# Attention outputs placed inside a retention visit, and other PSUM banks for the first and last batch

## The chip, the cores and the metric

The kernel runs on one core of a Trainium2 chip. What is measured is the device time of one execution in microseconds (us). The engines are named as in the profile: PE is TensorE (matmuls), PEld its weight loads, DVE is VectorE, ACT is ScalarE, POOL is GpSimd, and SP issues the DMAs. Matmul results lie in PSUM, which has 8 banks; everything else lies in SBUF.

## What is computed

Three stages run over 8 batches of 576 positions, all in float32. Cut to what matters, the reference is:

```
# retention: 8 heads of 64
ret = (q @ k.T) / 8 * D           # D[i,j] = gamma**(i-j) for i >= j, else 0
x = (ret @ v)                      # laid out as (8, 576, 512)
# mixture of attentions: 4 experts, the best 2 of each position are kept
logits = x @ w_gate
for e in range(4):
    a = softmax(causal(x @ wq[e] @ (x @ wk[e]).T / 8))
    ye = a @ (x @ wv[e]) @ wo[e]
    out += (gate weight of e at this position, or 0) * ye
# token and channel mixing
theta = out @ w_theta
y = w_tok_r @ (out * cos(theta)) + w_tok_i @ (out * sin(theta))
u = out + y
return u + relu(u @ w_ch)
```

## The kernel before

**First half** (to about 485 us). Retention is done in chunks of 128 positions, each of two blocks of 64. A visit, `ret_step(b, c, nx)`, does the late part of chunk c and the early part of the next chunk: `ret_scores` (line 134), `ret_state` (line 150: the running state, summed in the one PSUM bank `pS`, which ACT copies to S in line 153 after each block) and `ret_values` (line 163, and in line 170 the query products, which read S). All these are 64x64 matmuls on the four quarters of the array; a "diag" list (scores and states) and an "off" list (values) are taken one by one in turn, so that neighbours run at the same time. The state of an even block is the last of the diag list. It adds to pS, so it can't start before ACT has copied pS after the odd block before it.

The main loop goes through 80 units of attention (8 batches, 2 pairs of experts, 5 row tiles). A unit does `at_scores` (line 304), softmax on DVE and ACT (lines 307 and 312) and `at_trans` (line 351; DVE and ACT copy the result to PT in lines 356 and 358). `at_out` (line 370) multiplies PT with V for a group of row tiles, and ACT copies that to ob (line 374). A table, `SLOTS`, names the retention visits R1 to R5 to the next batch, made in 5 of the 10 units of a batch; the outputs that are due (`outs`) come behind a visit, in R1, R3, R4 and R5. The order of PE in this half is the order in which the code is written; the other engines' order is made by a scheduler.

At the end of the first half `token_tile` makes x2 and theta for tiles of 128 positions (lines 547 to 552; k, then nr = k minus theta in line 552, whose operand lies in pS or a w bank), and `load_o` loads the attention's outputs and multiplies them with the gate on POOL (line 520).

**Second half.** A scheduler orders all engines. `z_tile` makes z from nr for one tile and one half of the columns: three small DVE instructions (absolute value in line 564, minus pi/2 in line 565, clamp in line 566), one Sin on ACT over both halves of the tile (line 567), a product with x2 on DVE (line 569), and a split into a rounded part zh (ACT, line 103) and a rest zl (DVE, line 104). `mix(b, h)` multiplies z with the token weights TK: 108 matmuls of line 711 per half into four banks called acc, each 256 or 320 columns wide (`TS`). DVE copies or adds the banks to u (line 725 for batch 0, 723 for others), ACT makes the rounded uh (line 726), POOL or DVE the rest ul (line 727). `channel(b, et)` makes 24 matmuls for each of four blocks et (lines 98 to 100) into four banks called w, and DVE applies relu and adds to u (line 740). The loop over b also calls `x_put` (a DVE transpose, line 751, and DMAs) and `x_get` (DMAs), which lay x out anew for u.

PSUM holds, in the second half, 4 acc banks and 4 w banks. Where batch 0 goes from half 0 to half 1, half 1 has to wait until half 0 has been read out of acc.

## Time and profile before

| | us |
|---|---|
| median of 3 runs | 912.73 |
| lowest and highest | 907.61, 915.47 |
| the profiled execution | 907.77 |
| its span, first to last instruction | 905.8 |
| PE busy | 863.0 |
| DVE busy | 628.8 |
| ACT busy | 454.9 |
| POOL busy | 218.9 |

A timeline row gives the start in us from the span's start, the length in us, engine, line, operation, what is written <- what is read, how many like instructions in a row it stands for (xN), and in brackets the idle time ahead of it on its engine with what ended it. Matmuls follow each other before the one ahead has ended, so the time of a row xN is not the sum of its parts. The clock is the granted TensorE clock as a share of its full 2.4 GHz.

### The profile page before, as it was taken

To read this page: it belongs to the slowest core of one execution; us is meant where nothing else is said; L and a number is where in the kernel's file an instruction comes from. 1 tells how busy PE (TensorE), PEld (TensorE's weight loads), DVE (VectorE), ACT (ScalarE), POOL (GpSimd) and SP (SyncE) were. 2 spreads that over 40 slices of the span, in tenths; PEclk is the share of its full clock that TensorE was granted. 3 is DMA by queue.
4 is the path that set the end of the run, shared out by engine and by line. 5 is a ranking of instruction groups with operands and counts; after the bars stand their busy time and mean duration, and the time that the engine had idled before them with its cause. 6 is when DMAs were issued, how large, how long until landed. Compare 5 with 4: busy or idle time off the path is not lost.

```text
span 905.8 us, 25503 instructions
## 1 busy us (share of the span) xinstructions
PE 863.0 (95%) x10062; PEld 803.9 (89%) x10062; DVE 628.8 (69%) x1779; ACT 454.9 (50%) x1198; POOL 218.9 (24%) x268
## 2 busy tenths in 40 slices
PE   6998999899999999998999989999999999999998
PEld 6987888788898888888878889999999999999998
DVE  5376767878787776777769947866578764676732
ACT  2466666666666665665656513443244533434320
POOL 2434152452535434242212102001020110001010
PEclk8999999999999999999999999999999999999999
DMA  7857566676667667656795152333425123251401
GB/s 276 237 143 234 159 203 170 187 223 184 194 182 241 167 180 227 163 148 207 202 317 173 30 143 50 62 90 92 128 50 135 35 72 80 37 125 25 106 23 53
DMA packets 146216, 130.30 MB, mean 144 GB/s; under 512 B 83504, under 2 KB 121648, under 8 KB 146096
## 3 DMA queue, kind: packets, MB, share of 16 engines
q1 hardware_dynamic: 145952, 128.39, 50.1%
q8 instruction: 79, 1.29, 0.6%
q0 software_dynamic: 144, 0.28, 0.2%
q14 instruction: 41, 0.34, 0.1%
HBM read 78.03 MB, written 32.00 MB: 121 GB/s over the span
## 4 chain that ended last, share of the span: by engine, by line
PE 67%; DVE 10%; DMA 8%; ACT 6%; issue 3%; POOL 2%; SPq 2%; DVEq 0%; ACTq 0%; POOLq 0%
PE acc L711 22%; PE w L99 9%; PE w L98 9%; PE w L100 9%; PE w L242 4%; PE w L370 4%; PE w L304 3%; DMA kv<-kv 3%; PE w L351 2%; ACT P L312 2%; PE pS L150 2%; DVE P L307 1%; DMA TK<-td 1%; DMA wst<-w 1%; ACT U L225 1%
## 5 line engine op out<-in xcount | busy, mean ns | idle before, releaser
L711 PE MATMUL acc<-TK,zh 128*128 128x256 f32 (+1 forms) x1024 | 180.7, 299 | 3.4 <-ACT zh L103 1.8
L711 PEld LDWEIGHTS acc<-TK,zh 128*128 128x128 f32 x1024 | 155.7, 191 | 4.0 <-issue 3.7
L312 ACT ACTIVATE P<-P,st 128x128 f32<-128x128 f32 (+4 forms) x160 | 95.6, 598 | 55.9 <-DVE st L307 55.5
L711 PE MATMUL acc<-TK,zl 128*128 128x256 f32 (+1 forms) x512 | 110.9, 298 | 0.0
L727 POOL TENSOR_TENSOR ul<-u,uh 128x576 fp32r<-128x576 f32 x16 | 24.3, 1540 | 336.4 <-ACT uh L726 336.4
L307 DVE CUSTOM_DVE_ANT_0 P<-w,cm 128x128 f32<-128x128 f32 (+4 forms) x160 | 71.8, 477 | 24.4 <-PE w L304 24.1
L711 PEld LDWEIGHTS acc<-TK,zl 128*128 128x128 f32 x512 | 87.0, 191 | 0.0
L103 ACT ACTIVATE zh<-cs 128x512 fp32r<-128x512 f32 x64 | 40.4, 631 | 90.2 <-PE acc L711 68.2
L99 PE MATMUL w<-xl,WH 128*128 128x288 f32 x256 | 75.9, 296 | 4.5 <-POOL xl L183 4.5
L567 ACT ACTIVATE cs<-cs 128x512 f32<-128x512 f32 x72 | 45.2, 631 | 69.1 <-DVE cs L565 55.2
L98 PE MATMUL w<-uh,CH 128*128 128x256 f32 (+1 forms) x256 | 75.5, 297 | 2.4 <-ACT uh L726 2.4
L98 PE MATMUL w<-xh,WH 128*128 128x288 f32 x256 | 76.0, 297 | 0.7 <-ACT PT L356 0.7
L104 DVE TENSOR_TENSOR zl<-cs,zh 128x512 fp32r<-128x512 f32 x64 | 44.0, 690 | 46.4 <-ACT zh L103 45.7
L304 PE MATMUL w<-KK,U 128*64 128x288 f32 (+4 forms) x384 | 76.2, 327 | 0.0
L99 PE MATMUL w<-ul,CH 128*128 128x256 f32 (+1 forms) x256 | 75.7, 296 | 0.0
L100 PE MATMUL w<-uh,CH 128*128 128x256 f32 (+1 forms) x256 | 75.6, 296 | 0.0
L100 PE MATMUL w<-xh,WL 128*128 128x288 f32 x256 | 75.4, 295 | 0.0
L150 PE MATMUL pS<-vp,kv 64*64 64x64 f32 x1024 | 44.0, 226 | 19.8 <-ACT S L153 15.9
L442 POOL TENSOR_TENSOR r<-r,ex 128x192 f32<-128x192 f32 (+1 forms) x51 | 29.5, 579 | 136.4 <-ACT hl L443 61.8
L569 DVE SCALAR_TENSOR_TENSOR cs<-cs,x 128x512 f32<-128x512 f32 x72 | 48.7, 687 | 18.6 <-ACT cs L567 18.4
L304 PEld LDWEIGHTS w<-KK,U 128*128 128x128 f32 (+1 forms) x384 | 53.9, 171 | 7.5 <-issue 4.3
L150 PEld LDWEIGHTS pS<-vp,kv 64*64 64x64 f32 x1024 | 35.8, 137 | 27.1 <-ACT S L153 18.5
(140 smaller groups left out, 2267.2 us busy)
## 6 DMA issues: line engine op xcount, KB each, us to landing
KK<-KN SPq DMA_DIRECT2D x128, 144.0 KB
kt<-qk SPq DMA_DIRECT2D x32, 512.0 KB
kv<-kv SPq DMA_DIRECT2D x32, 512.0 KB
raw<-wd SPq DMA_DIRECT2D x43, 192.0 KB
xd<-xb SPq DMA_DIRECT2D x126, 64.0 KB
out<-u SPq DMA_DIRECT2D x28, 288.0 KB
u<-xd SPq DMA_DIRECT2D x28, 288.0 KB
td<-hl SPq DMA_DIRECT2D x27, 192.0 KB
```

Source lines behind the costliest of these rows:

```text
L98: nc.tensor.matmul(ps, ah, bh, start=first, stop=False)
L99: nc.tensor.matmul(ps, ah, bl, start=False, stop=False)
L100: nc.tensor.matmul(ps, al, bh, start=False, stop=last)
L103: nc.scalar.activation(h, src, AF.Copy)
L104: nc.vector.tensor_sub(l, src, h)
L150: nc.tensor.matmul(pS[half(s), x, :], u[half(s), j, 0, x * D:x * D + D], vp[half(s), j, x, :], start=k == 0 and x == 0, stop=False, skip_g ...
L304: nc.tensor.matmul(ps[s][:R], U[:, s, rs], KK[:, s, x, j0:j1], start=x == 0, stop=x == 1)
L307: MARK["dve"] = nc.vector.tensor_tensor_reduce(Ps[s][:R, j0:j1], ps[s][:R], cm[:R, o + j0:o + j1], 1.0, st[:R, 0, s:s + 1] if i else 3.0e3 ...
L312: MARK["act"] = nc.scalar.activation(Ps[s][:R, :n], Ps[s][:R, :n], AF.Exp, bias=st[:R, last, s:s + 1], scale=-1.0, accum_out=SUM[p][:R, m, ...
L567: nc.scalar.activation(cs, cs, AF.Sin)
L569: nc.vector.scalar_tensor_tensor(z, cs, -1.0, x2[:, None, ds].to_broadcast([128, 2, 256]), op0=OP.mult, op1=OP.mult)
L711: nc.tensor.matmul(acc[d][j], A[:, dc], TK[:, kt, W, t0:t1], start=q == 0 and n == 0, stop=q == 8 and n == 2)
```

## The change

Line numbers in the diff are left out; the file after the change is some 3 to 17 lines longer above the places in question (line 150 becomes 153, 370 becomes 377, 711 becomes 725).

1. `ret_step` takes a function `mid`. In the loop's visits it does 12 steps of the off list beside the diag list without the even state, then calls `mid`, which does the due `at_out`s, and then the even state beside the rest of the off list. Without `mid` (the visits ahead of the loop) the even state now comes after the whole off list.
2. `z_tile` does no subtraction on DVE. The Sin is two instructions of 256 columns each, and the first takes minus pi/2 as a bias from a tile `quarter`.
3. The POOL multiply of `load_o` depends on the latest relu of `channel` recorded when it is written.
4. Banks of 288 and 288 columns (`TH`) instead of 256 and 320, but for mix of batch 0. In batches 0 and 7 mix half 1 writes the w banks and channel the acc banks.
5. In batch 0 `x_put` is written behind the channel blocks and `x_get(1)` at the end.

```diff
 TS = [(0, 256), (256, 576)]
+TH = [(0, 288), (288, 576)]
...
+    quarter = consts.tile([128, 1], F32, name="quarter")
+    nc.vector.memset(quarter, -math.pi / 2.0)
...
         if nx[0] < B:
             loads(*nx)
 
-    def ret_step(b, c, nx):
+    def ret_step(b, c, nx, mid=None):
 
         diag, off = [], []
         if 0 <= c < NCH - 1:
             diag.append(ret_state(b, 2 * c + 1))
         if nx:
             diag.append(ret_scores(*nx))
-            if nx[1] < NCH - 1:
-                diag.append(ret_state(nx[0], 2 * nx[1]))
         if c >= 0:
             off.append(ret_values(b, c))
-        for _ in zip_longest(chain(*diag), chain(*off)):
+        last = nx and nx[1] < NCH - 1
+        off = chain(*off)
+        for _, _ in zip_longest(chain(*diag), islice(off, 12) if last and mid else off):
+            pass
+        if mid:
+            mid()
+        for _ in zip_longest(ret_state(nx[0], 2 * nx[1]) if last else (), off):
             pass
 
 
...
-        nc.gpsimd.tensor_mul(OL[b], OL[b], gw)
+        m = nc.gpsimd.tensor_mul(OL[b], OL[b], gw)
+        if "ch" in MARK:
+            tc.add_manual_dep(m.ins, MARK["ch"].ins.name, mybir.DependencyInfo(
+                mybir.DependencyClass.Sync, mybir.DependencyReason.DATA), reason="behind the channel products")
...
         cs = zp.tile([128, 2, 256], F32, name="cs", bufs=2)
         nc.vector.tensor_scalar(cs[:, 0, :].bitcast(I32), nr[:, ds].bitcast(I32), 0x7FFFFFFF, None, op0=OP.bitwise_and)
-        nc.vector.tensor_scalar(cs[:, 0, :], cs[:, 0, :], math.pi / 2.0, None, op0=OP.subtract)
         nc.vector.tensor_scalar(cs[:, 1, :], nr[:, ds], PI_LO, -PI_LO, op0=OP.min, op1=OP.max)
-        nc.scalar.activation(cs, cs, AF.Sin)
+        nc.scalar.activation(cs[:, 0, :], cs[:, 0, :], AF.Sin, bias=quarter)
+        nc.scalar.activation(cs[:, 1, :], cs[:, 1, :], AF.Sin)
...
             if between[:1] == "R":
                 c = int(between[1])
                 x = b + 1
-                ret_step(x, c - 1, (x, c) if c < NCH else (x + 1, 0) if x + 1 < B else None)
-                for o in outs:
-                    at_out(*o)
-                outs = []
+                def mid():
+                    for o in outs:
+                        at_out(*o)
+                    outs.clear()
+
+                ret_step(x, c - 1, (x, c) if c < NCH else (x + 1, 0) if x + 1 < B else None, mid)
         else:
             work(b, between)
             for o in outs:
...
     def mix(b, h):
         g, w = divmod(b, 2)
         tiles = [0, 1, 2, 3, 4] if w == 0 else [4, 5, 6, 7, 8]
-        acc = [[ps2.tile([128, t1 - t0], F32, name=f"acc{d}{i}", bufs=1, padded_shape=[128, 512])
-                for i, (t0, t1) in enumerate(TS)] for d in range(2)]
+        ts = TH if b else TS
+        spare = h and b in EDGE
+        acc = [[ps2.tile([128, t1 - t0], F32, name="w" if spare else f"acc{d}{i}", bufs=4 if spare else 1,
+                         padded_shape=[128, 512]) for i, (t0, t1) in enumerate(ts)] for d in range(2)]
...
     TAIL = {}
+    EDGE = (0, B - 1)
 
     def channel(b, et):
         uh, ul = UT[b]
         u = XU[b]
         es = slice(et * C, et * C + C)
-        for t0, t1 in TS:
-            ps = ps2.tile([128, t1 - t0], F32, name="w", bufs=4, padded_shape=[128, 512])
+        for j, (t0, t1) in enumerate(TH):
+            spare = b in EDGE
+            ps = ps2.tile([128, t1 - t0], F32, name=f"acc{et % 2}{j}" if spare else "w", bufs=1 if spare else 4,
+                          padded_shape=[128, 512])
             for kt in range(4):
                 mm3(ps, CH[:, kt, 0, es], CH[:, kt, 1, es], uh[:, kt, t0:t1], ul[:, kt, t0:t1], kt == 0, kt == 3)
             o = u[:, et, t0:t1]
-            nc.vector.scalar_tensor_tensor(o, ps, 0.0, o, op0=OP.max, op1=OP.add)
+            MARK["ch"] = nc.vector.scalar_tensor_tensor(o, ps, 0.0, o, op0=OP.max, op1=OP.add)
...
         for x in q[:2]:
             if x not in X2:
                 token_tile(ps2, *x)
-            x_put(*x)
+            if b:
+                x_put(*x)
         mix(b, 1)
         for x in q[2:]:
             if x not in X2:
                 token_tile(ps2, *x)
-            x_put(*x)
-        if b + 1 < B:
+            if b:
+                x_put(*x)
+        if 0 < b < B - 1:
             x_get(b + 1)
         for et in range(4):
             channel(b, et)
+            for x in q[2 * et:2 * et + 2] if not b else []:
+                x_put(*x)
+        if not b:
+            x_get(1)
     ps2.release()
     wk.release()
     zp.release()
```

**PE in the first R1 visit.** The rows are the end of the pairs (the off list's query products w<-kt,S beside scores w<-kt), the even state (pS<-vp,kv) and the outputs (w<-PT,V). Before:

```order
L170 MATMUL w<-kt,S_134 64x64 x2
L134 MATMUL w<-kt 64x64 x2
L170 MATMUL w<-kt,S_134 64x64 x2
L150 MATMUL pS<-vp,kv 64x64 x8
L370 MATMUL w<-PT,V 64x128 x2
L370 MATMUL w<-PT,V 64x256 x4
L370 MATMUL w<-PT,V 64x128 x2
```

After:

```order
L173 MATMUL w<-kt,S_136 64x64 x2
L137 MATMUL w<-kt 64x64 x2
L173 MATMUL w<-kt,S_136 64x64 x2
L377 MATMUL w<-PT,V 64x128 x2
L377 MATMUL w<-PT,V 64x256 x4
L377 MATMUL w<-PT,V 64x128 x2
L153 MATMUL pS<-vp,kv 64x64 x8
```

The outputs have moved from behind the eight state matmuls to ahead of them; the pairs ahead of both are the same.

**PE in batch 0, from mix half 0 to half 1.** acc00 to acc11 and w are PSUM tiles, the number behind a name tells one use of a bank from the next. Before:

```order
L711 MATMUL acc10_8973<-TK_8449,ztl_9002 128x256
L711 MATMUL acc11_8974<-TK_8449,ztl_9002 128x320
L711 MATMUL acc00_9151<-TK_8449,zh_9161 128x256 x2
L711 MATMUL acc00_9151<-TK_8449,zl_9162 128x256
L701 MATMUL acc00_9151<-ident_119,x2_8524 128x128
L711 MATMUL acc01_9152<-TK_8449,zh_9161 128x320 x2
L711 MATMUL acc01_9152<-TK_8449,zl_9162 128x320
```

After:

```order
L725 MATMUL acc10_8975<-TK_8451,ztl_9004 128x256
L725 MATMUL acc11_8976<-TK_8451,ztl_9004 128x320
L725 MATMUL w_9143<-TK_8451,zh_9153 128x256
L725 MATMUL w_9144<-TK_8451,zh_9153 128x320
L725 MATMUL w_9143<-TK_8451,zh_9153 128x256
L725 MATMUL w_9144<-TK_8451,zh_9153 128x320
L725 MATMUL w_9143<-TK_8451,zl_9154 128x256
```

Half 1 has moved from the acc banks, which half 0 has just filled, to w banks. The transposes of x (line 701) that stood between stand later.

**DVE at the start of the second half.** nr<-k,pS is the line that reads pS last (552 before, 562 after); cs is a z tile in the making (564 to 569 before, 574 to 579 after). Before:

```order
L552 TENSOR_TENSOR nr_8880<-k_8877,w_8868 128x512
L104 TENSOR_TENSOR zl_8943<-cs_8936,zh_8942 128x512
L569 SCALAR_TENSOR_TENSOR cs_8946<-cs_8946,x2_8563 128x512
L550 TENSOR_SCALAR k_8918<-k_8918 128x512
L564 TENSOR_SCALAR cs_8975<-nr_8609 128x256
L552 TENSOR_TENSOR nr_8921<-k_8918,pS_8909 128x512
```

After:

```order
L562 TENSOR_TENSOR nr_8882<-k_8879,w_8870 128x512
L579 SCALAR_TENSOR_TENSOR cs_8938<-cs_8938,x2_8526 128x512
L560 TENSOR_SCALAR k_8920<-k_8920 128x512
L562 TENSOR_TENSOR nr_8923<-k_8920,pS_8911 128x512
L107 TENSOR_TENSOR zl_8945<-cs_8938,zh_8944 128x512
L579 SCALAR_TENSOR_TENSOR cs_8948<-cs_8948,x2_8565 128x512
L574 TENSOR_SCALAR cs_8977<-nr_8611 128x256
```

The zl, one product and one absolute value that stood ahead of nr<-k,pS now follow it; the product ahead of the zl, which stood further up, is now next to it.

Of the six multiplies of line 520 for batches 2 to 7, the program before has two ahead of batch 0's subtractions of line 727 on POOL and the other four one by one between the batches' subtractions. After the change batch 0's subtractions come first, and all six multiplies stand one by one behind them.

## Rows read from the trace of the kernel before

**Rows 1.** page, engines: busy us (share of the span), instructions

```profile
PE 863.0 (95%) x10062; PEld 803.9 (89%) x10062; DVE 628.8 (69%) x1779; ACT 454.9 (50%) x1198; POOL 218.9 (24%) x268
```

**Rows 2.** windows: us; busy of PE, PEld, DVE, ACT, POOL; clock; DMA

```profile
484.80:488.30 3.50, 3.50 (x15) 3.48 (x16) 3.19 (x10) 2.40 (x4) 0.00 (x0) 0.51 0.74 189
502.00:526.00 24.00, 19.97 (x149) 19.27 (x148) 22.95 (x51) 11.96 (x21) 3.25 (x2) 1.00 0.20 33
505.00:520.00 15.00, 15.00 (x115) 14.77 (x114) 14.34 (x31) 7.26 (x13) 3.20 (x2) 1.00 0.21 36
535.00:850.00 315.00, 315.00 (x2137) 302.08 (x2136) 217.93 (x490) 126.19 (x229) 29.24 (x16) 1.00 0.32 77
```

**Rows 3.** PE's waits: line <- releaser: us, times, longest

```profile
PE pS L150 <- ACT S L153: 15.9, 19, 2.6
```

**Rows 4.** timeline, start of the second half: PE, ACT, DVE

```profile
484.76 1.20 PE L711 MATMUL acc<-TK,zh 128*128 128x256 f32 x4 [1.79 <-ACT zh L103]
...
483.59 0.31 ACT L374 COPY ob<-w 128x192 f32<-128x192 f32 x1
...
483.88 0.68 DVE L552 TENSOR_TENSOR nr<-k,pS 128x512 f32<-128x512 f32 x1
```

**Rows 5.** timeline, DVE and PE around mix half 1, batch 0

```profile
503.34 1.54 DVE L725 COPY u<-acc 128x256 f32<-128x256 f32 x4
...
503.91 0.47 PE L711 MATMUL acc<-TK,zh 128*128 128x256 f32 x2 [1.63 <-DVE u L725]
...
521.72 1.54 DVE L725 COPY u<-acc 128x256 f32<-128x256 f32 x4
...
523.30 0.39 PE L98 MATMUL w<-uh,CH 128*128 128x256 f32 x1 [2.40 <-ACT uh L726]
```

**Rows 6.** timeline, PE at mix half 1, batch 7

```profile
874.54 0.51 PE L711 MATMUL acc<-TK,zth 128*128 128x256 f32 x2 [1.52 <-DVE u L723]
```

**Rows 7.** timeline, PE in the first and last R1 visit

```profile
56.49 0.68 PE L150 MATMUL pS<-vp,kv 64*64 64x64 f32 x16 [0.62 <-ACT S L153]
...
57.10 1.52 PE L370 MATMUL w<-PT,V 128*64 128x128 f32 x16
...
381.50 0.68 PE L150 MATMUL pS<-vp,kv 64*64 64x64 f32 x16 [0.56 <-ACT S L153]
```

**Rows 8.** timeline, ACT in the first R1 visit

```profile
55.88 0.27 ACT L358 COPY PT<-w 128x128 f32<-128x128 f32 x1
...
56.03 0.40 ACT L153 ACTIVATE S<-pS 128x256 f32<-128x256 f32 x1
```

**Rows 9.** timeline, R3 visits: DVE, ACT, PE; PE in the last

```profile
178.43 0.20 DVE L358 COPY PT<-w 64x64 f32<-64x64 f32 x1
...
178.86 0.39 ACT L153 ACTIVATE S<-pS 128x256 f32<-128x256 f32 x1
...
179.30 0.27 PE L150 MATMUL pS<-vp,kv 64*64 64x64 f32 x2 [2.12 <-ACT S L153]
...
286.88 0.27 PE L150 MATMUL pS<-vp,kv 64*64 64x64 f32 x2 [0.39 <-ACT S L153]
```

**Rows 10.** timeline, PE and DVE in an R5 visit

```profile
85.78 1.30 PE L370 MATMUL w<-PT,V 128*64 128x256 f32 x12
...
85.88 0.29 DVE L358 COPY PT<-w 128x128 f32<-128x128 f32 x1
```

**Rows 11.** groups by form: xcount | busy us, mean ns | idle

```profile
L565 DVE TENSOR_SCALAR cs<-cs 128x256 f32<-128x256 f32 x72 | 20.4, 283 | 0.0
L567 ACT ACTIVATE cs<-cs 128x512 f32<-128x512 f32 x72 | 45.2, 631 | 69.1 <-DVE cs L565 55.2 <-DVE cs L566 13.7
L103 ACT ACTIVATE oh<-ol 128x256 fp32r<-128x256 f32 x32 | 13.1, 416 | 11.4 <-PE w L99 9.7 <-PE pS L99 1.4 <-POOL ol L520 0.2
```

**Rows 12.** timeline, POOL and DVE in batch 0

```profile
490.39 2.69 POOL L520 TENSOR_TENSOR ol<-ol,og 128x1152 f32<-128x1152 f32 x1 [12.70 <-DMA og<-gd]
...
491.05 2.18 DVE L564 TENSOR_SCALAR cs<-nr 128x256 int32<-128x256 int32 x1
```

More of the change, by code (lines that the diff above doesn't have):

```diff
@@ L3 @@
 from contextlib import ExitStack
-from itertools import chain, zip_longest
+from itertools import chain, islice, zip_longest
 import concourse.bass as bass
@@ L709, in mix @@
                 for n, (A, W) in enumerate(((zh, 0), (zh, 1), (zl, 0))):
-                    for j, (t0, t1) in enumerate(TS):
+                    for j, (t0, t1) in enumerate(ts):
                         nc.tensor.matmul(acc[d][j], A[:, dc], TK[:, kt, W, t0:t1], start=q == 0 and n == 0,
@@ L720, in mix @@
             k = 2 * h + d
-            for j, (t0, t1) in enumerate(TS):
+            for j, (t0, t1) in enumerate(ts):
                 if b:
```

## The prediction

> **What bounds the kernel now.** I read the page's engine line first: PE is busy 95% of the span, no other engine above 69% [rows 1]. Then windows: between 535 and 850 us, where most of the second half lies, PE is busy for 315.00 of 315.00 us [rows 2], so nothing that ACT, DVE or POOL do faster or slower there shows until it makes PE wait. A gain must therefore come out of PE's idle time, and the list of PE's waits says where that is: the largest item is line 150 (the state product) waiting for ACT's copy S of line 153, 15.9 us in 19 places [rows 3]. The remaining waits of interest are single ones, around the two edges of the second half: 1.79 us before the first line 711 at 484.76 [rows 4], 1.63 at 503.91 and 2.40 at 523.30 in batch 0 [rows 5], 1.52 at 874.54 in batch 7 [rows 6]. The last thing read is PE's granted clock: 0.51 in the stretch behind 484.80, that is, the lower level of 1.2 GHz for about 3.5 us, right after the wait of 1.79; it stays 1.00 around the waits of batch 0 [rows 2].
>
> **The change, part by part.**
>
> *Outputs inside the visit.* The copy S cannot start until the last pair of matmuls into pS has ended, and the next state product cannot start until S is copied. The change puts at_out's products into that hole. At visit R1 the pairs end at 55.87, S is copied from 56.03 to 56.43, the 16 state rows start at 56.49 after 0.62 us, and the 16 rows of line 370 follow at 57.10 for 1.52 us [rows 7, 8]. With the two swapped, the 1.45 us of line 370 cover the copy entirely. Its own PT tiles: ACT's last copy (line 358) ends at 56.15 [rows 8], the second group needs it only for its last rows, so I charge nothing. There are 7 such visits, from 0.62 at 56.49 to 0.56 at 381.50 [rows 7], about 0.57 each: **−4.0**. At R3 three visits wait, 2.12 us at 179.30 being the first and 0.39 at 286.88 the last [rows 9]. There the S copy is late (178.86 to 179.25) because ACT and DVE are late as a whole, and the PT copies that at_out needs are just as late: DVE's second ends at 178.63 [rows 9], and ACT makes its own right ahead of S. So at_out can start some 0.35 us before S is ready, and that is about what a visit gains: **−1.0** for the three; the bound on the other side is 4.17 less a remainder, say −2.5. At R5 no such wait stood, and at_out now starts 0.57 us sooner, where one of its copies (DVE line 358, 85.88 to 86.17) ends only after line 370 began at 85.78 [rows 10]: up to 0.2 in some of the 7 visits, **+0.5**, between 0 and 1.4. R2 has no outputs to move and R4 no last state; their order on PE is the same, so R2's seven waits of about 0.6 stay. The two prologue visits lose the pairing of the even state product with other rows (16 rows alone take 0.68 us [rows 7]): up to +0.7 each, but those visits wait on loads, so I take 0. First half: **−4.5** (−6.5 to −2.5).
>
> *Start of the second half.* The first line 711 is said to wait for ACT's zh; really its bank is freed last by DVE's line 552, which reads pS until 484.56, ACT's ob copy being done at 483.90 [rows 4]. In the new order three DVE instructions that stood between the two lines 552 (a zl, a line 569, a line 564) come after the second, the subtraction is gone (72 of 283 ns [rows 11], 0.20 us of pitch each), and POOL's multiply no longer runs beside DVE's line 564. What that beside costs is seen at 491: a line 564 that starts 0.66 us after POOL's line 520 takes 2.18 us instead of the usual 0.28 [rows 12]; another such pair stands at 475. ACT's own chain through k bounds what comes of it: **−0.6** (−0.3 to −1.0).
>
> *z tiles.* The Sin of 128x512 (631 ns) becomes two of 128x256. The nearest row for such a size is line 103's 416 ns [rows 11], so two take between 0.63 and 0.83 us. DVE saves 0.20 us per tile, ACT's part of the ring gets up to 0.20 longer; where the ring is the limit, that cancels. In the steady stretch both lie under PE: ACT is busy 126 of 315 us, DVE 218 [rows 2]. **0**.
>
> *Banks.* In batch 0, PE ends mix half 0 at 502.28 (503.91 less its wait) and waits for DVE's four copies out of acc, which begin only at 503.34 [rows 5]. With half 1 in the w banks this wait goes: **−1.6**. But DVE is busy 14.34 of the 15 us from 505 to 520 [rows 2]: from the first four copies to the next four it needs 18.4 us (503.34 to 521.72), and from there to the uh that PE waits for it is 1.6 more (523.30). PE needs 17.0 us from the start of half 1 to the end of the 8 channel rows that can do without that uh (503.91 to 523.30 less 2.40) [rows 5]. DVE's new path, by the order: the same three transposes and eight copies, both POOL subtractions of line 727 still beside it, 14 small z instructions of 0.20 us pitch for 18 (−0.8), but one more product and one more zl of 0.6 each (+1.2), and fewer short waits for ACT since tiles now go in pairs (−0.9 at best). That is 17.9 to 18.8; I keep 18.4. The copies now start when PE ends, not 1.1 us later, so the uh wait grows from 2.40 to 18.4+1.6−17.0 = 3.0 us: **+0.6**. In batch 7 the wait of 1.52 at 874.54 [rows 6] goes in the same way and DVE has time there: **−1.5** (−1.0 to −1.5).
>
> *The clock.* Full speed behind the start of the second half is worth 3.5 x 0.49 = 1.7 us: four rows of line 711 take 1.20 us there [rows 4]. A shorter wait may end that stretch; a wait of 3.0 us at the channel may begin a new one. Row for row, 1.79 us of waiting was followed by the lower level and 1.63 and 2.40 were not [rows 2, 4, 5], so length alone does not decide. I take it that one of the two stretches remains: **0** (−1.7 to +1.7). The Trainium skill, "TensorE: Matmul & The Clock Gate", section "Loop structure matters more than you think", says that a copy of results out of PSUM between tiles does not cool TensorE. By that rule the longer channel wait costs only itself, and the sum would be 1.7 us lower; the trace agrees for the waits of batch 0, and disagrees at 484.76, where the bank was also freed by copies.
>
> *Multiply behind the channel.* DVE's splits of the loaded tile now wait for a POOL multiply that starts after the channel's last relu: 2.7 us of POOL [rows 12] and the hops, some 3.5 us in which DVE stands in order, at three boundaries. DVE is idle 97 of 315 us [rows 2], about 16 per batch: **0**. Halves of 288 against 256/320 have the same columns and cost PE nothing. The loads of `x_get(1)`, now issued behind batch 0's channel, are read only after batch 1's mix half 0, a whole half of 108 matmuls later: **0**.
>
> **Sum.** −4.5 −0.6 −1.6 +0.6 −1.5 +0 = −7.6 us. On the profiled execution of 907.77 us that is 900.2. That execution lies at the low end of the three runs (907.61, 912.73, 915.47); the mean of the four is 910.9, and from it I get 903.3.
>
> **Rivals.**
> 1. *Both half-clock stretches go, and DVE keeps up* (batch 0's DVE path at about 16 us instead of 18.4, the POOL clashes of [rows 12] being gone): −1.7 more, up to −2 more for the uh wait, R3 at its full −2.5: −9.3 to −12, about 900. For it: two of the three pauses above kept the clock. Against: DVE's 14.34 of 15 us. The rule of the Trainium skill named above would give its clock part.
> 2. *Gain eaten at batch 0*: the half clock stays at 484.8 and comes a second time behind the 3.0 us wait (+1.7), R5 and the prologue cost their bounds (+1.8): −3.5 to −5, about 907. For it: DVE is the last to arrive there already.
> 3. *Slower*: the multiply behind the channel. If z tiles were ready less than 3.5 us ahead of PE, DVE's standing would go through to PE; each of six multiplies in the loop could cost up to 2.7, 16.4 us, less the 7.6: 920. It decides where the ring's lead falls under 3.5 us; the 315.00 busy of 315.00 with DVE at 69% speaks against it.
>
> **How the numbers follow.** Forecast 0.48 (−5.5 to −9: 902 to 905.5 from the mean), rival 1 0.30, rival 2 0.17, rival 3 0.05. The range takes rival 1 with the start point 2 us lower (897) and rival 2 with it as far higher (910). About 1%, 9.1 us, is what a measurement of this kernel can tell from no change. Faster by over 1% is rival 1 and a little of the forecast: 0.35; within 1%: 0.60; slower: 0.05.
>
> **What the new profile would show.** Right: line 150 waits for S only at R2 (about 4.7 us) and in the prologue; line 370 starts at the end of the pairs at R1; no wait at mix half 1 of batches 0 and 7; one uh wait of about 3 us in batch 0; no line 564 stretched beside line 520. Wrong: a new wait of line 370 for PT at R1, R3 or R5 above 0.5 us a visit; PE below 100% between 535 and 850; a second stretch at the lower clock; PE's first line 711 still 1.8 us late.

## The result, and the profile after

The changed kernel takes 899.75 us (median of 4 runs, 896.38 to 902.51); the kernel before 911.06 in the same comparison. The ratio is 0.9875 with a 95% interval of 0.9843 to 0.9907. A second comparison (6 runs of it, 29 of before) gave 0.9904 (0.9877 to 0.9931). So it is faster by about 1%, on the edge of what the prediction called a difference: 9 to 11 us, where the sum said 7.6.

The two profiled executions differ by less: spans of 905.8 and 899.6 us, 6.2 apart. The engine line after the change, to be set against [rows 1]:

```profile
PE 864.2 (96%) x10062; PEld 804.5 (89%) x10062; DVE 614.8 (68%) x1708; ACT 466.0 (52%) x1270; POOL 219.2 (24%) x268
```

DVE lost 14 us of work and ACT gained 11, as the z tiles' edit says, and none of that is the gain: PE's busy time is the same within 1.2 us, and the span shrank by what PE no longer waits. The list of PE's waits after, against [rows 3] (line, releaser: us in total, times, longest):

```profile
PE pS L153 <- ACT S L156: 9.6, 11, 2.7
PE w L377 <- DVE PT L363: 6.3, 6, 1.7
PE acc L101 <- ACT uh L740: 3.3, 1, 3.3
PE w L102 <- POOL xl L186: 2.9, 5, 1.1
PE w L249 <- POOL xl L186: 2.5, 2, 2.4
```

The line that the second of these answers to, in the trace of before:

```profile
PE w L370 <- DVE PT L356: 1.6, 3, 0.7
```

The wait for S fell from 15.9 to 9.6 us. At_out (now line 377) waits 6.3 us for DVE's PT copies, where it waited 1.6 before: 3.9 of the 6.3 are new waits at R3 (0.59, 1.59 and 1.74 us), the rest stands in the last batch, where the 1.6 stood. The third line is batch 0's uh wait, 2.40 before. Where the time went is best seen by where PE begins each stage, read off the first matmul of the stage in the two timelines:

| PE begins | before, us | after, us | won in the stage ahead |
|---|---|---|---|
| mix of batch 0 (line 711, now 725) | 484.76 | 480.95 | 3.81 |
| mix of batch 1 | 535.19 | 531.33 | 0.05 |
| mix of batch 2 | 590.43 | 586.12 | 0.45 |
| mix of batch 7 | 858.47 | 853.69 | 0.47 |
| channel of batch 7 | 889.04 | 882.49 | 1.77 |
| end of the span | 905.8 | 899.6 | −0.35 |

Batch 0, to which the prediction gave a gain of 1.0 us, gave nothing in this pair of traces. In a second pair (runs 12 and 1 below) it takes 51.64 and 50.64 us, so between none and all of that 1.0 came.

**R1** went as predicted. PE in the first visit, to be set against [rows 7]:

```profile
56.51 1.53 PE L377 MATMUL w<-PT,V 128*64 128x128 f32 x16
57.97 0.68 PE L153 MATMUL pS<-vp,kv 64*64 64x64 f32 x16
```

Neither row has an idle time ahead of it: the outputs start where the pairs end and cover the copy. Over the 7 visits PE's place moves forward by 0.63 to 0.69 us each.

**R3 and R5** (the rows that answer to [rows 9] and [rows 10]): PE and DVE in batch 2's R3, then in batch 0's R5.

```profile
178.75 2.08 PE L377 MATMUL w<-PT,V 128*64 128x192 f32 x18 [1.59 <-DVE PT L363]
178.61 0.21 DVE L365 COPY PT<-w 64x64 f32<-64x64 f32 x1
...
86.09 1.34 PE L377 MATMUL w<-PT,V 128*64 128x256 f32 x12
86.65 0.29 DVE L365 COPY PT<-w 128x128 f32<-128x128 f32 x1
```

At R3 the wait of 2.12 us for S has become one of 1.59 for PT. At R5 a PT copy ends at 86.94, well after the outputs began at 86.09, and the 12 rows take 1.34 us instead of 1.30. From the scores ahead of the visit to the next PE needs 0.16 to 0.20 us more in 6 of the 7 batches (the last visit makes no product into pS). Most of that is not the copy. In the R5 visits of batches 1 and 5 the outputs wait for no copy, and 0.16 us are lost all the same. Batch 1, from the last pair to the next scores, before and after:

```profile
138.42 0.23 PE L170 MATMUL w<-kt,S 64*64 64x64 f32 x2
138.47 0.63 PE L150 MATMUL pS<-vp,kv 64*64 64x64 f32 x16
139.03 1.30 PE L370 MATMUL w<-PT,V 128*64 128x256 f32 x12
140.26 1.27 PE L304 MATMUL w<-KK,U 128*64 128x288 f32 x8
...
139.65 0.23 PE L173 MATMUL w<-kt,S 64*64 64x64 f32 x2
139.80 1.30 PE L377 MATMUL w<-PT,V 128*64 128x256 f32 x12
141.03 0.68 PE L153 MATMUL pS<-vp,kv 64*64 64x64 f32 x16
141.65 0.61 PE L311 MATMUL w<-KK,U 128*64 128x288 f32 x3
```

The state products used to follow the pairs, which have the same 64x64 form, after 0.05 us; the outputs, of another form, follow them after 0.15. The state products behind the outputs then take 0.62 us to the next start instead of 0.56. Those two steps are the 0.16.

**Batch 0.** PE at the start of the second half and at the channel, and DVE's first and last copies, against [rows 4] and [rows 5]; below them two windows with the columns of [rows 2]:

```profile
480.95 0.89 PE L725 MATMUL acc<-TK,zh 128*128 128x256 f32 x5 [0.49 <-ACT ob L381]
496.50 1.54 DVE L739 COPY u<-acc 128x256 f32<-128x256 f32 x4
515.48 1.54 DVE L739 COPY u<-w 128x256 f32<-128x256 f32 x4
517.06 0.61 PE L101 MATMUL acc<-uh,CH 128*128 128x288 f32 x1 [3.33 <-ACT uh L740]
```

```profile
515.80:522.60 6.80, 5.54 (x23) 5.54 (x24) 4.40 (x11) 2.19 (x4) 0.00 (x0) 0.50 0.00 0
535.00:850.00 315.00, 315.00 (x2143) 302.09 (x2142) 215.05 (x450) 139.54 (x288) 31.98 (x17) 1.00 0.35 80
```

The first wait is down from 1.79 to 0.49 us, the wait in the middle is gone, and the stretch at 1.2 GHz that stood behind 484.80 is gone. But from the first copies to the last DVE needs 18.98 us (18.38 before), the uh wait is 3.33 us, and from the end of that wait PE runs at half speed for 5.5 us, some 2.8 lost. The steady stretch is full, as before.

### The profile page after: what moved, and what is told of

Same layout as the page of the kernel before. It is cut to its first block, busy times and chain, and to the rows that moved or that the text cites. A ratio compares the mean times of both kernels' runs of the same rounds, so it can differ in the third digit from the quotient of the medians.

```text
span 899.6 us, 25474 instructions
## 1 busy us (share of the span) xinstructions
PE 864.2 (96%) x10062; PEld 804.5 (89%) x10062; DVE 614.8 (68%) x1708; ACT 466.0 (52%) x1270; POOL 219.2 (24%) x268
## 4 chain that ended last, share of the span: by engine, by line
PE 78%; DMA 8%; DVE 6%; POOL 3%; ACT 2%; issue 2%; SPq 1%; POOLq 0%; ACTq 0%; DVEq 0%
PE acc L725 22%; PE w L102 10%; PE w L101 10%; PE w L103 9%; DMA kv<-kv 5%; PE w L311 5%; PE w L377 4%; PE w L249 4%; PE w L358 4%; PE pS L153 2%; PE w L725 2%; PE w L137 1%; POOL xl L186 1%; PE w L173 1%; PE acc L101 1%
## 5 line engine op out<-in xcount | busy, mean ns | idle before, releaser
L725 PE MATMUL acc<-TK,zh 128*128 128x288 f32 (+2 forms) x896 | 155.8, 296 | 0.5 <-ACT ob L381 0.5
L725 PEld LDWEIGHTS acc<-TK,zh 128*128 128x128 f32 x896 | 131.9, 189 | 0.8 <-issue 0.6
L725 PE MATMUL acc<-TK,zl 128*128 128x288 f32 (+1 forms) x448 | 95.8, 295 | 0.0
L725 PEld LDWEIGHTS acc<-TK,zl 128*128 128x128 f32 x448 | 72.3, 189 | 0.0
L576 ACT ACTIVATE cs<-cs,quarter 128x256 f32<-128x256 f32 x72 | 36.4, 506 | 60.1 <-DVE cs L574 57.2
L377 PE MATMUL w<-PT,V 128*64 128x192 f32 (+3 forms) x576 | 56.6, 325 | 6.8 <-DVE PT L363 6.3
L358 PE MATMUL w<-ident,P 128*128 128x128 f32 (+2 forms) x480 | 58.8, 257 | 0.0
L153 PE MATMUL pS<-vp,kv 64*64 64x64 f32 x1024 | 45.9, 227 | 12.7 <-ACT S L156 9.6
L377 PEld LDWEIGHTS w<-PT,V 128*64 128x64 f32 (+1 forms) x576 | 36.3, 135 | 24.0 <-DVE PT L363 7.1
L122 POOL TENSOR_TENSOR vp<-kv,gam 128x512 f32<-128x512 f32 (+1 forms) x40 | 38.6, 966 | 74.0 <-DMA kv<-kv 59.7
```

Source lines behind the costliest of these rows:

```text
L153: nc.tensor.matmul(pS[half(s), x, :], u[half(s), j, 0, x * D:x * D + D], vp[half(s), j, x, :], start=k == 0 and x == 0, stop=False, skip_g ...
L358: nc.tensor.transpose(tp[:w, j, :], Ps[s][:R, j * C:j * C + w], ident[:R, :R])
L377: nc.tensor.matmul(po[s * 64:s * 64 + 64, c0:], V[:ROWS[j], j, 2 * p + s, :], v, start=j == 0, stop=j == last, skip_group_check=True)
L725: nc.tensor.matmul(acc[d][j], A[:, dc], TK[:, kt, W, t0:t1], start=q == 0 and n == 0, stop=q == 8 and n == 2)
```

## The experiments

All were timed against the kernel before on the same chip, and ratios below are to it. Runs 1 to 4 and 12 share one chip, 5 to 8 a second, 9 to 11 a third, so a ratio says more across these groups than a median.

**1. The changed kernel again.**

> The changed kernel once more, timed against the kernel before. The two profiled executions differ by 6.2 us in span (905.8 and 899.6), the medians by 11.3. Theory: both kernels spread by several us from execution to execution, among other things by whether TensorE's lower clock comes behind a wait in batch 0 (2.8 us in the profiled one), and the profiled pair is a low one of before and a high one of after; more rounds then give a ratio of 0.988 to 0.992, and this profile shows a uh wait of about 3.3 us in batch 0 again, with or without the clock stretch behind it. Rival: the change is worth the 6 us of the profiled pair and the medians were luck: 0.993 or higher.

Measured: 900.07 us, ratio 0.9904 (0.9877 to 0.9931). Its trace has the uh wait again (3.34 us) with the half clock behind it. Both traced executions of the changed kernel (901.38 and 902.62 us) lie near the top of their sets, whose mean is 899.9. So the pair of traces may show less than the change is worth. From the first line 711 to the end of the span the changed kernel takes 418.7 us in one trace and 418.9 in the other, the kernel before 421.1 (422.3 in run 12): the second half repeats well, and most of the spread lies in the first.

**2. The first part alone.** The edit is the diff's `ret_step` and loop.

> The kernel before with the first part of the change alone: outputs inside the visit. Theory: at each R1 0.6 us is won (4.4 in all), the start loses about 0.7 because two visits ahead of the loop no longer pair the even state, R5 loses about 0.2 a visit to PT copies, R3 wins little; the second half's first line 711 comes 2.5 us earlier than before less the part that the banks' end of the first half adds, and the total is 2 to 3 us lower, ratio 0.997. Rival: the outputs hide the S copies everywhere at no cost, 7 to 8 us lower, ratio 0.992.

Measured: 904.5 us, ratio 0.9968 (0.9949 to 0.9987), 2.9 us: the theory's size. Its second half begins with the waits of before (1.95, 1.65 and 2.40 us). In its trace line 711 (there 717) begins at 479.74, 5.0 us earlier than before, twice the theory's 2.5: one trace of the first half does not give the part's size.

**3. The banks alone.**

```
-        acc = [[... name=f"acc{d}{i}", bufs=1 ... for i, (t0, t1) in enumerate(TS)] ...]
+        spare = h and b in EDGE
+        acc = [[... name="w" if spare else f"acc{d}{i}", bufs=4 if spare else 1 ...]]
```

> The kernel before with the other banks in batches 0 and 7 alone (columns 256 and 320 as before). Theory: batch 7 gives 1.5 to 1.8 us, batch 0 at most 1, since DVE sets its pace: the wait of 1.63 goes and the uh wait grows from 2.4 to 3 to 4.5 us, and a stretch at the lower clock may come behind it and take the rest: total -0.5 to -2.8 us. Rival: both waits are won, 3.2 us, and the uh wait stays at 2.4.

Measured: 908.24 us, ratio 0.9999 (0.9981 to 1.0017). PE at batch 0's channel:

```profile
523.60 0.58 PE L98 MATMUL acc<-uh,CH 128*128 128x256 f32 x1 [7.00 <-ACT uh L727]
```

Without the other edits the uh wait is 7.00 us, far more than I thought, with the half clock in and behind it. DVE's copies out of half 0 begin at 503.64, 3.8 us after PE has ended half 0 (499.85); PE no longer waits for them there, and the lateness reaches it at the channel. Batch 0 is 2.8 us longer in this trace, batch 7 1.8 shorter.

**4. The z tiles alone.**

```
-        nc.vector.tensor_scalar(cs[:, 0, :], cs[:, 0, :], math.pi / 2.0, None, op0=OP.subtract)
-        nc.scalar.activation(cs, cs, AF.Sin)
+        nc.scalar.activation(cs[:, 0, :], cs[:, 0, :], AF.Sin, bias=quarter)
+        nc.scalar.activation(cs[:, 1, :], cs[:, 1, :], AF.Sin)
```

> The kernel before with the changed z tile alone (no subtraction on DVE, Sin in two halves with a bias). Theory: hidden under TensorE everywhere but at the start of the second half (up to 0.5 us earlier) and in batch 0, where DVE's path from the first copies to the last gets shorter by up to 1 us and the uh wait with it: -0.5 to -1.5 us. Rival: the longer Sin in the ring cancels it, no difference; or, ACT being later at the start of the second half, up to 1 us slower.

Measured: 908.0 us, ratio 0.9986 (0.9964 to 1.0009), not to be told from no change. In its trace PE goes from the last scores of the first half to line 711 in 10.82 us, as in every trace of a kernel with the new z tile, against 12.10 before and 11.74 in run 12: the gain at the start of the second half, 0.9 to 1.3 us, is the z tiles' own. In batch 0 it only shifts the wait to the middle (3.88 us for the copies, with the half clock in and behind it; no uh wait).

**5. Batch 0's transposes made late.**

```
+        tr = nc.vector.transpose(xb, X2[g, i])
+        if late: tc.add_manual_dep(tr.ins, MARK["ch"].ins.name, ...)
```

> The changed kernel with batch 0's five transposes of x really made behind the channel (each depends on the relu ahead of it), where the scheduler had left them in the mix halves. Theory: DVE sets the pace of batch 0; its path from the first copies out of mix half 0 to the last of half 1 loses three transposes of 0.65 us, 19.0 to about 17.0 us, the uh wait falls from 3.3 to about 1.4 us and no stretch at the lower clock follows (2.8 us in both profiles of the changed kernel): 4 to 5 us below the changed kernel, ratio to the kernel before about 0.985. Rival: uh comes late because of ACT or of PE's own order; the wait stays near 3.3 us, no gain; or the transposes only move the wait into batch 1, whose u is loaded later.

Measured: 902.74 us, ratio 0.9929 (0.9904 to 0.9954), no gain. My theory fell here. DVE lost the three transposes but needed 18.83 us from copies to copies, nearly as before. What it did instead:

```profile
511.24 0.69 DVE L107 TENSOR_TENSOR zl<-cs,zh 128x512 fp32r<-128x512 f32 x1 [0.35 <-ACT zh L106]
513.61 0.69 DVE L107 TENSOR_TENSOR zl<-cs,zh 128x512 fp32r<-128x512 f32 x1 [0.55 <-ACT zh L106]
517.97 0.69 DVE L579 SCALAR_TENSOR_TENSOR cs<-cs,x 128x512 f32<-128x512 f32 x1 [0.48 <-ACT cs L577]
```

It waits for ACT's half of each z tile: 2.0 us in that stretch against 0.65 in the changed kernel, and one more product of a later tile stands ahead of the copies. And batch 1 pays as the rival said, since its u is laid out later (it takes 59.45 us against 54.79; the traced execution, 909.29 us, is the slowest of its 12):

```profile
562.84 1.03 PE L725 MATMUL acc<-TK,zth 128*128 128x288 f32 x4 [2.30 <-DVE u L737]
```

**6. The banks in batch 7 alone** (`EDGE = (B - 1,)`).

> The changed kernel with the other banks in batch 7 alone; batch 0 keeps acc for both halves. DVE's order around batch 0 is the same as in the changed kernel. Theory: in batch 0 the banks win nothing but move PE's wait from the middle (about 1.6 us, behind the copies) to the end, where it is long enough for the lower clock; without them the copies end at the same time, the waits are about 1.6 and 1.7 us, and no stretch at 1.2 GHz follows: 2 to 3 us faster than the changed kernel, ratio to the kernel before about 0.988. Rival: the banks of batch 0 are worth their 1.6 us: 1.6 us slower than the changed kernel, ratio 0.992 to 0.993.

Measured: 899.03 us, ratio 0.9891 (0.9852 to 0.9931): no difference to the changed kernel, and neither theory nor rival was right on how. PE in the middle of batch 0 and at its channel, then the whole of batch 0:

```profile
493.23 0.87 PE L725 MATMUL acc<-TK,zh 128*128 128x256 f32 x4
...
513.22 0.61 PE L101 MATMUL w<-uh,CH 128*128 128x288 f32 x1 [2.85 <-ACT uh L740]
...
477.10:527.70 50.60, 47.60 (x333) 46.69 (x334) 39.18 (x85) 23.91 (x51) 3.25 (x2) 0.93 0.36 96
```

With the acc banks the middle wait is under 0.2 us too (the row has no bracket). So it was not the banks that took the 1.63 us away; the copies now begin when PE ends, since DVE is no longer late there (run 8 shows why). The uh wait is 2.85 us, the half clock comes all the same, and batch 0 is 50.6 us long, as in the changed kernel.

**7. Outputs inside at R1 alone**, the visits ahead of the loop paired as before.

```
-                ret_step(x, c - 1, ..., mid)
+                ret_step(x, c - 1, ..., mid, between == "R1")   # else the even state stays in the diag list
```

> The changed kernel with the outputs inside the visit at R1 alone; at R3 and R5 they stand behind the visit again, and the two visits ahead of the loop pair the even state as before. Theory: R1 is where the gain is; R5 gets back about 0.2 us in each of 7 visits, R3 loses up to 0.35 in three, the start gets back about 0.7: 1 to 2 us below the changed kernel at the start of the second half. Rival: R3 and R5 are needed too: 1 to 2 us slower.

Measured: 902.17 us, ratio 0.992 (0.9896 to 0.9944): not faster, if anything slower. R3 with the outputs behind:

```profile
178.36 0.37 PE L153 MATMUL pS<-vp,kv 64*64 64x64 f32 x2 [2.43 <-ACT S L156]
```

Two R3 waits were 2.4 us here (1.59 and 1.74 inside), and a stretch at half clock came with each. Against the changed kernel's trace PE loses 4.0 us at these two visits and gets back the 1.1 of R5. But the kernel before, which has the same order there, waited 2.12 and 1.66 us at the full clock in its first trace; in run 12's the half clock came with the first of them, 2.25 us. So how much of the 4.0 belongs to the order stays open.

**8. POOL's multiply without its dependence.** `tc.add_manual_dep(m.ins, ...)` is taken out.

> The changed kernel without the dependence of POOL's multiply on the channel: two multiplies run on POOL ahead of batch 0's subtractions again. Theory: each holds a DVE instruction up for about 1.9 us (line 564 took 2.2 instead of 0.28 us beside one), DVE sets batch 0's pace, so the uh wait grows from 3.3 to about 5 us and the second half begins up to 0.5 us later: 1.5 to 2.5 us slower than the changed kernel. Rival: DVE has that time left while it waits for PE ahead of the copies: no difference.

Measured: 902.75 us, ratio 0.9932 (0.9909 to 0.9956), some 2.5 us slower than the changed kernel's 0.9904, though the two intervals overlap. In the trace batch 0 takes 52.42 us against 50.38, and the uh wait is what the theory said and more:

```profile
494.43 0.69 PE L722 MATMUL w<-TK,zh 128*128 128x256 f32 x4
497.38 1.54 DVE L736 COPY u<-acc 128x256 f32<-128x256 f32 x4
...
517.30 0.61 PE L101 MATMUL acc<-uh,CH 128*128 128x288 f32 x1 [5.91 <-ACT uh L737]
```

The first two rows show where it comes from. The copies out of half 0 begin 2.95 us after PE has begun half 1; in the changed kernel they begin 0.27 us before it (496.50 and 496.77). From copies to copies DVE needs 18.34 us, no more than there. So it is this dependence that has DVE's copies ready in the middle of batch 0.

**9. The copies ahead of z tiles that are not needed yet.**

```
         zt = nc.vector.tensor_scalar(cs[:, 0, :].bitcast(I32), ...)
+        if (g, i, h) in ((0, 7, 0), (0, 8, 0)):
+            tc.add_manual_dep(zt.ins, MARK["u"].ins.name, ...)   # batch 0's last copy of half 1
```

> The changed kernel with one order on DVE changed: the z tiles of token tiles 7 and 8 for batch 1 depend on the last copy out of batch 0's mix half 1, so two z tiles that PE does not need yet no longer stand ahead of the four copies it waits for. The run without the three transposes there had the same 18.8 us from copies to copies, with DVE waiting for zh and cs in between, so the earlier theory (the amount of DVE's work sets the pace) fell. Theory now: the copies are late because z tiles for the next batch stand ahead of them, each a round trip of DVE, ACT, DVE; with two fewer the path falls from 19.0 to about 15.5 us, the uh wait from 3.3 to about 0.6 us, and no stretch at the lower clock follows: 2.7 + 2.8 = 5 us below the changed kernel, ratio to the kernel before about 0.985. Rival: the uh wait is set by the way from copy to uh to PE (1.6 us after the copies begin) and by z tiles then missing in batch 1: no more than 1 us.

Measured: 897.12 us, ratio 0.9887 (0.9852 to 0.9922). DVE's last copies, PE's channel behind them, and the whole of batch 0:

```profile
513.31 1.62 DVE L742 COPY u<-w 128x256 f32<-128x256 f32 x4
...
514.90 0.53 PE L101 MATMUL acc<-uh,CH 128*128 128x288 f32 x2
...
482.40:527.00 44.60, 44.52 (x333) 43.96 (x334) 39.07 (x85) 24.05 (x51) 3.25 (x2) 1.00 0.41 108
```

The path is 15.27 us, the uh wait is gone (no bracket), the clock stays at 1.00, and batch 0 takes 44.4 us from its first line 711 (482.49) to batch 1's (526.93), against 50.4: 5.9 us. Of this 0.4 is given back in batch 1. By the trace the rival (no more than 1 us) is out, and from the first mix to the end of the span it takes 413.1 us, in run 10's trace too, against 418.7 and 418.9. The timed runs do not settle it: 0.9887 lies between the changed kernel's two ratios, 0.9904 and 0.9875. What the order took away from ahead of the copies is work; windows with the columns of [rows 2], from copies to copies, in the changed kernel and here:

```profile
496.50:515.48 18.98, 17.23 (x130) 16.77 (x128) 18.07 (x39) 12.14 (x26) 3.25 (x2) 1.00 0.24 39
498.04:513.31 15.27, 15.27 (x117) 15.04 (x116) 14.55 (x30) 9.06 (x19) 3.25 (x2) 1.00 0.22 35
```

DVE's busy time falls by 3.5 us and the path by 3.7: DVE has hardly any idle time on it in either.

**10. The same, R5's outputs behind the visit, the start paired.**

> The kernel of the run just named, with outputs inside the visit at R1 and R3 only; at R5 they stand behind it, and the visits ahead of the loop pair the even state. Theory: R5 got slower by about 0.2 us in each of 7 visits, since at_out came before its copies; that and up to 0.7 at the start come back, while R3 keeps its shorter wait (2.4 us there with outputs behind, 1.6 to 1.7 with them inside): 1 to 2 us below the run just named. Rival: what R5 loses is taken back by the wait for POOL's xl that follows it: no difference.

Measured: 895.1 us, ratio 0.9863 (0.9837 to 0.9889), the lowest ratio; 2 us below the run before it, as the theory had it, though within the intervals, and run 11, with R5's outputs inside, has as low a median. In the trace every R5 visit takes as long as before the change again, which gives 1.1 us; by the rows shown above that is the change of form, and not the PT copies of the theory.

**11. The same as 9 with acc banks in batch 0.**

> The first kernel of this call with the acc banks in batch 0 again (other banks in batch 7 alone). Theory: with the copies in time, the w banks of batch 0 are worth only what PE waits at the start of half 1, about 0.4 to 0.5 us, as in the run with batch 7 alone: 0.5 us slower than that kernel at most. Rival: they are worth the 1.6 us that the trace of before shows there.

Measured: 894.88 us, ratio 0.9875 (0.9841 to 0.9909). Its mix of batch 0 takes 32.04 us against 31.56 in run 9: by the traces the banks of batch 0 are worth 0.5 us, the theory's figure. The times cannot show it; this median is 2 us below run 9's.

**12. The kernel before, a second trace.**

> The kernel before, unchanged, as a second trace of it. The parts read off the traces add up to 6 to 7 us, the timed comparison gives 8.7 and 11.3. Seven traces of kernels whose first half is that of the changed kernel start the second half between 477.1 and 484.9 us. Theory: the kernel before spreads in the same way, by the loads that POOL and then PE wait for in the first half and by the lower clock behind such waits, and its one trace (484.76) was a low one: this one starts the second half at 486 to 489, and the stretch from there to the end of batch 0's channel is 50.5 us again. Rival: it starts at 484 to 485 again, and the 2 us lie elsewhere.

Measured: ratio 0.9996 (0.9974 to 1.0018). The theory about the first half fell: line 711 begins at 484.35, like the first trace's 484.76. Batch 0 differs, though:

```profile
484.35 0.77 PE L711 MATMUL acc<-TK,zh 128*128 128x256 f32 x4 [1.43 <-ACT zh L103]
504.73 0.55 PE L711 MATMUL acc<-TK,zh 128*128 128x256 f32 x1 [4.40 <-DVE u L725]
524.10 0.38 PE L98 MATMUL w<-uh,CH 128*128 128x256 f32 x1 [1.07 <-ACT uh L726]
```

The wait in the middle is 4.40 us here and was 1.63 there, with the uh wait the smaller (1.07 for 2.40); the half clock comes with the one in the middle. Half 0 runs at the full clock here and takes 15.98 us, where it took 17.51 behind the half clock at 484.80; so PE comes to the copies earlier and waits longer. I read the two waits as one lateness of DVE, paid early or late; no run shows that by itself.

## Why the prediction was right, and where not

The time, 899.75, lies in the range, and the sign, R1, the start of the second half and batch 7 were right; R3, R5 and the banks of batch 0 were not, or not for the reason given. It is rival 1's figure (about 900) rather than the forecast's 903.3, but not by rival 1's way: DVE did not keep up in batch 0, and the half clock came. Of the signs that I had named as wrong, one came: waits for PT above 0.5 us at R3. Step by step:

- *R1, −4.0*: right; 7 visits, 4.5 us.
- *R3, −1.0*: wrong. At_out waits for PT nearly as long as the state had waited for S (3.9 us for 4.2). In the trace 0.34 us came at the 2.12 wait, as I had worked out for it, but 0.27 was lost at the next one (1.66 us for S, now 1.74 for PT), and at batch 1, where the state had not waited for S at all, a new wait of 0.59 costs 0.66. I had looked only at the visits where S was late, and not at when DVE makes PT in the others. The term is a loss of about 0.6. Run 7, with waits of 2.4 us at R3 and the half clock with them, speaks for leaving the outputs inside there all the same, but does not show it.
- *R5, +0.5*: undersized, and for another reason; 0.16 to 0.20 in 6 visits is 1.1, near the bound of 1.4. PT copies, my reason, are 0.04 us in 4 visits and nothing in 2. The 0.16 in each is what the new order of the two forms of matmul takes, which I had put at nothing. Run 10 gets it back.
- *The start, 0*: not settled. The first scores come 0.7 us later in one trace and 0.3 earlier in another, since those visits wait on loads.
- *Start of the second half, −0.6*: undersized; the wait went from 1.79 to 0.49, 1.3 us, beyond my bound of 1.0 (from 1.43, 0.9, in run 12's trace of before). Run 4 shows that the z tiles alone give all of it, and run 8 that it stays without POOL's dependence, one of my reasons.
- *Banks in batch 0, −1.6 and +0.6*: the sizes of the two waits came as predicted (none, 3.33 for 3.0; path 18.98 for 18.4), the causes did not. The middle wait would have gone without the banks (run 6); it is POOL's dependence that has the copies ready there (run 8). And I took DVE's path as given. It is the work that stands ahead of the copies in DVE's order, and two of its z tiles are for the next batch: run 9 put them behind the copies, and the path fell by 3.7 us, the uh wait and the half clock went. Taking away just any work does not do: run 5 took out three transposes, and DVE waited for ACT's part of the z tiles instead.
- *The clock, 0*: one stretch remained, as I took it, but the new one cost about 2.8 us and the old one 1.7. That takes back what the waits of batch 0 gave. The old one does not stand in every trace of the kernel before either: in run 12's the clock stays up at the start and falls at the middle wait. The Trainium skill ("TensorE: Matmul & The Clock Gate", section "Loop structure matters more than you think") says that a copy out of PSUM between tiles does not cool TensorE in a loop where the next tile's matmuls follow immediately. I had applied it to a PE that stands and waits for such copies, which it does not speak of: here each uh wait of 2.85 to 7.00 us had the half clock in or behind it.
- *Batch 7, −1.5*: right, 1.77.
- *The multiply behind the channel, 0*: right for the danger (315.00 of 315.00 busy), but I had not counted that batch 0 needs it: without it batch 0 is 2.0 us longer in run 8's trace.
- *Columns, 0*: 0.09 us a batch are won from batch 2 to 6, where only the columns differ on PE; batch 1 won 0.45 us that I did not foresee.

Two slips of the working changed nothing: six times 2.7 is 16.2 and not 16.4, and rival 1's additions come to −12.8 and not −12.

By traces the parts add up to 6.2 (5.8 in the pair of runs 12 and 1), by the timed runs to 9 to 11. That the forecast of 7.6 lies between them is in part luck: R3, R5 and batch 0 gave 3 us less than their terms, and R1, the start, batch 1 and batch 7 some 2 us more. The traced executions of the changed kernel, 901.38 and 902.62 us, lie some 2 us above the mean of their sets, 899.9; that part of the difference lies in which executions were traced, and what took longer in them stays open, as the others left no trace. Nor do the parts add up alone: runs 2, 3 and 4 gave 2.9, 0 and 1.3 us in ratio, and the whole 9. The likely reason is that the banks, the z tiles and POOL's order each take away a part of one lateness in batch 0, so that each alone only moves it; POOL's order was not timed alone on the kernel before, nor any two together, so this is argued.

## What to carry to other kernels

Before a wait is moved by a free bank, ask what the late engine does ahead of the instruction that is waited for: if it is work for later, reorder it there, and the wait goes instead of moving. An instruction moved forward into a hole can only start when its own operands are there; look up when they are made, at every place it is moved. And where parts of a change act on one lateness, time them together: alone they may show nothing.

## What the runs showed of the hardware

- A wait of PE can cost more than itself. In or just behind the uh waits of 2.85, 2.94, 3.33, 3.34, 3.60, 5.91 and 7.00 us, the middle waits of 3.88 and 4.40 and batch 1's of 2.30 the granted clock fell to 0.50; with the one of 1.07 and those of 1.52 to 1.65 us in batches 0 and 7 it did not. Between them it is open: it fell behind 1.79 and 1.95 us at the start of the second half and not with 2.40 at the channel, or 1.43 and 1.53 at the start.
- A small DVE instruction that takes 0.28 us elsewhere took 1.5 us beside POOL's subtractions. In the changed kernel two such stand on batch 0's path from copies to copies:

```profile
498.11 3.25 POOL L741 TENSOR_TENSOR ul<-u,uh 128x576 fp32r<-128x576 f32 x2 [43.11 <-ACT uh L740]
498.56 1.53 DVE L574 TENSOR_SCALAR cs<-nr 128x256 int32<-128x256 int32 x1
500.01 1.51 DVE L575 TENSOR_SCALAR cs<-nr 128x256 f32<-128x256 f32 x1
```

  That is up to 2.5 us of the 18.98; no run moved the subtractions, so what they cost is open.
- Executions with the same order of PE's first half (the changed kernel twice, runs 5, 6, 8, 9 and 11) begin the second half between 477.11 and 484.90 us. In part it is loads: POOL's line 122 waits for a DMA, POOL's xl stands behind it, and PE waits for xl. In one of them:

```profile
88.54 1.04 POOL L122 TENSOR_TENSOR vp<-kv,gam 128x512 f32<-128x512 f32 x1 [3.01 <-DMA kv<-kv]
89.54 0.73 POOL L186 TENSOR_TENSOR xl<-xt,xh 128x256 fp32r<-128x256 f32 x1
90.32 0.40 PE L102 MATMUL w<-xl,WH 128*128 128x288 f32 x1 [2.07 <-POOL xl L186]
```

The same wait is 0.91 us in the changed kernel's trace. Differences of 2 us between single traces of this first half mean nothing.
